# A gated mix of a convolution and a linear attention: data spectrum and parameters in memory of their own, attention values scaled in bf16 from on-chip memory, first query exponentials inside the key loop

## The chip, the cores and the metric

The kernel runs on one core of one Trainium2 chip. The metric is device time in microseconds; of three runs of the kernel before the change the median was 410.11 (406.83 to 412.22). The core's engines are named as in the profile: PE is TensorE's matrix multiply, PEld its weight load, DVE is VectorE, ACT is ScalarE, POOL is GpSimd, and SP is the engine whose queue issues the transfers. SBUF is the on-chip memory, PSUM the accumulators that PE writes, DRAM the memory off the core.

## The reference, cut to what matters

With x of 2048 rows and 512 channels, the output is `g*a + (1-g)*b`:

```python
g = sigmoid((x * gate_w).sum(-1, keepdims=True))
# a: a long convolution along the rows, per channel d
K = einsum("dn,dnl,dn->dl", Cc, exp(dt*A * l), dt*Bc).real      # n = 128 states, l = 0..2047
a = irfft(rfft(pad(x)) * rfft(pad(K)))[:2048] + x * Dskip
# b: linear attention, 32 heads of 16
q, k, v = x @ wqkv
phi(t) = concat(softmax(t @ w_phi), softmax(-(t @ w_phi)))
kv = einsum("hsf,hsd->hfd", phi(k), v);  z = phi(k).sum(s)
b = (phi(q) @ kv / (phi(q) @ z + 1e-6)) @ wo
```

Here `dt = exp(log_dt)`, and `A`, `Bc`, `Cc` are complex, each from two 512x128 inputs.

## The kernel before, in words

Every stage is written out in Python, with tiles taken from pools; the framework's scheduler then fixes one issue order for each engine, places the tiles, and puts in the semaphore waits. An engine works through its list in that order: an instruction that waits holds up everything behind it on its engine.

**The front.** SP loads two parameters (`Are`, `Aim`), `log_dt`, then the data as `UD` (four transfers, L738), four more parameters, the small vectors, the qkv weights `wraw` (L747) and `wo_sb` (L748). `build_fft_consts` builds the twiddle tables `TB` and `W1`, and from `TB` by transposes on PE (L151) the inverse table `TI`; `build_selectors` builds `selE`. `compute_rates` takes the decay rates through DRAM (`pz`, `stat`). `turn_x` transposes the data to `xT`. `compute_polar` makes the tables `Ctab` and `Dtab`: products of the parameters, then logarithms and exponentials, then an arctangent and four rounds of `big_a`, `big_n`, `trg` (an argument reduced on DVE, an absolute value and two sines on ACT). `fold_projection` multiplies the key and the query weights with `w_phi` (`Wkp`, `Wqp`). `u_path` computes the data's spectrum `XU` in two halves: matmuls `psA` (L381), 8 evictions `XAu`, matmuls `psB` (L402), 8 evictions `XU`. The tile `XAu` lies in the pool `xau`, which is opened where `compute_polar`'s pool has been closed. `gates` makes the gate.

**The key loop**, eight calls of `key_step`, each for two blocks of 128 rows: `pk` matmuls (L576), four exponentials `Ek` on ACT, sums `Zk` on DVE, their logarithm and reciprocal on ACT, `vp` matmuls (L589), then on DVE `vr = vp * reciprocal` for both signs (L591), and 64 small matmuls `kvp` that accumulate over the loop. `fold_kv` turns the result into `Mw` (matmuls `ktp`, `mps`).

**The query blocks.** `query_exp` (matmuls `pq`, exponentials `Eq`) and `query_block` for four blocks of 512 rows: `zs`, a short chain of ACT and DVE steps (`lnZ`, `den`, `apm`), then four times `aexp` on PE, two products `Eq` on DVE, twelve matmuls `bps` (L680, L683), an eviction `bs` and its transfer to `bSd`.

**The convolution kernel and the Fourier blocks.** `kgen_tables(h)` (four `E`, a table load, four `cs`, a table load on ACT) and `kgen(h)` (per half six DVE products `A`, five `R`, 64 matmuls `kps`; then the eviction `KD`, 8 matmuls `psA`, two evictions `XA`) make one eighth of the channels, h = 0 to 7. Two of them feed one Fourier block `fft(Q)`, Q = 0 to 3, of four groups: 48 matmuls `psB` (L402), eviction `XK`, two DVE products `t`, 32 matmuls `psz` (L444), eviction `Z`. After every two groups `Z` goes to DRAM as `Zd` (L451), and comes back transposed as `ZT` (L455). `finish(Q)` makes two output tiles `psy`: two matmuls each from `bS` (L467), 32 from `ZT` (L471), a product `ot` on DVE, four transfers. `psB`, `psz` and `psy` share a PSUM pool `psF` of two buffers; `args`, `kps`, `psA` share `psP`, also two. The end of the program reads

```python
fft(0)
for Q in range(1, 4):
    for h in (2 * Q, 2 * Q + 1):
        if h + 1 < 8:
            tabs[h + 1] = kgen_tables(h + 1)
        kgen(h)
    fft(Q)
    finish(Q - 1)
finish(3)
```

Of the kernel before, what the change touches and what calls it, by code (L numbers as in the profile page):

```python
# [11 lines left out]
ALU = mybir.AluOpType  # L12
# [99 lines left out]
def build_fft_consts(nc, act, persist, tp, ps_pool, icol, ident):  # L112
# [3 lines left out]
    fc.TI = persist.tile([128, 16, 4, 64], BF16, name="TI")  # L116
# [28 lines left out]
    for h in range(4):  # L145
        ps = ps_pool.tile([128, 4, 2, 64], F32, name="tips", tag="pb")
        for r4 in range(4):
            for rpar in range(2):
                r = 2 * (4 * h + r4) + rpar
                for cs in range(2):  # L150
                    nc.tensor.matmul(ps[64 * rpar:64 * rpar + 64, r4, cs, :], lhsT=fc.TB[0:64, r, cs, :], rhs=ident[0:64, 0:64],  # L151
                                     start=True, stop=True, tile_position=(0, 64 * rpar))
        nc.vector.tensor_copy(out=fc.TI[:, 4 * h:4 * h + 4, 2:4, :], in_=ps[:])
    nc.vector.tensor_scalar(out=fc.TI[:, :, 0:2, :], in0=fc.TI[:, :, 2:4, :], scalar1=-1.0, scalar2=None, op0=ALU.mult)
# [11 lines left out]

def build_selectors(nc, persist, tp, icol):

    selE = persist.tile([128, 32, 64], BF16, name="selE")
    c32 = tp.tile([128, 32], F32, name="c32")  # L170
    iota_f(nc, c32[:], [[1, 32]])
    m32 = tp.tile([128, 32], BF16, name="m32")
    nc.vector.tensor_scalar(out=m32[:], in0=c32[:], scalar1=icol["p31"], scalar2=None, op0=ALU.is_equal)
    v64 = tp.tile([128, 64], F32, name="v64")
    iota_f(nc, v64[:], [[1, 64]])
    b64 = tp.tile([128, 64], BF16, name="b64")
    nc.vector.tensor_scalar(out=b64[:], in0=v64[:], scalar1=1.0, scalar2=-31.5, op0=ALU.mult, op1=ALU.add)
    nc.vector.tensor_tensor(out=selE[:], in0=m32[:].unsqueeze(2).to_broadcast([128, 32, 64]),
                            in1=b64[:].unsqueeze(1).to_broadcast([128, 32, 64]), op=ALU.mult)
    return selE  # L180
# [22 lines left out]
def compute_polar(nc, act, persist, tp, psP, rawd, ld_b, ident):  # L203
# [29 lines left out]
    for k, o in (("Are", are), ("Aim", aim)):  # L233
        ps = turned(psP.tile([128, W], F32, name=f"ps{k}", tag="pb"), k)
        nc.vector.tensor_tensor(out=o[:], in0=ps[:], in1=dt_[:], op=ALU.mult)
    m2 = T("m2"); s2 = T("s2")
# [187 lines left out]
def k_spectrum_inverse(nc, fc, XA, nd, tpool, XU, d0, Z, Zd, ZT, ps_pool, tag, ev, evz, ngr):  # L424

    ns = 512 // nd
    for rg in range(16 // ns):
        rh0 = rg * ns
        ps = fft_stage_b(nc, fc, ps_pool, XA, nd // 2, rh0, tag)
        XK = tpool.tile([128, ns, 2, nd], BF16, name="XK")  # L430
        ev(XK[:].rearrange("p s i (c e x) -> p (s i c) e x", e=2, x=16), ps[:].rearrange("p e s i (c x) -> p (s i c) e x", x=16))
        t12 = tpool.tile([128, ns, 2, nd], BF16, name="t12")
        t34 = tpool.tile([128, ns, 2, nd], BF16, name="t34")
        Us = XU[:, rh0:rh0 + ns, :, d0:d0 + nd]
        nc.vector.tensor_tensor(out=t12[:], in0=Us, in1=XK[:], op=ALU.mult)  # L435
        nc.vector.tensor_tensor(out=t34[:], in0=Us, in1=XK[:, :, ::-1, :], op=ALU.mult)
# [131 lines left out]
def key_step(nc, act, at, xT, Wkp, wraw, kwk, psA, kvp, s2):  # L568
# [12 lines left out]
    vr = kwk.tile([128, 2, 2, 16, 34], BF16, name="vr")  # L581
    act(out=Zk[:], in_=Zk[:], func=ACT.Ln)
    act(out=vr[:, :, :, :, 32:34], in_=Zk[:].rearrange("p u g (m h) -> p (u g) m h", h=2), func=ACT.Exp, scale=-1.0)
    for u in range(2):
# [3 lines left out]
        for kt in range(4):  # L588
            nc.tensor.matmul(vp[:], lhsT=xT[:, kt, ss], rhs=wraw[:, kt, 1024:1536], start=(kt == 0), stop=(kt == 3))  # L589
        for sg in range(2):  # L590
            nc.vector.tensor_tensor(out=vr[:, u, sg, :, 0:32].rearrange("p m (h e) -> p m h e", e=16),  # L591
                                    in0=vp[:].rearrange("p (m h e) -> p m h e", m=16, h=2),
                                    in1=vr[:, u, sg, :, 32:34].unsqueeze(3).to_broadcast([128, 16, 2, 16]), op=ALU.mult)
        for i in range(8):
            sg, m = i // 4, i % 4
            for pr in range(4):
                nc.tensor.matmul(kvp[32 * pr:32 * pr + 32, i, :], lhsT=Ek[:, u, sg, 128 * m + 32 * pr:128 * m + 32 * pr + 32],
                                 rhs=vr[:, u, sg, 4 * m + pr, :], start=(st == 0 and i == 0), stop=(st == 15),
                                 tile_position=(0, 32 * pr), skip_group_check=True)


def fold_kv(nc, at, kp, kvp, wo_sb, ident, psA, Mw):
# [3 lines left out]
    nc.vector.tensor_tensor(out=zj[:], in0=kvp[:, :, 32:34], in1=at.mask2[:].unsqueeze(1).to_broadcast([128, 8, 2]), op=ALU.mult)  # L606
    nc.vector.tensor_reduce(out=zcol[:], in_=zj[:], axis=mybir.AxisListType.X, op=ALU.add)
    for pr in range(4):
        rows = slice(32 * pr, 32 * pr + 32)
        nc.vector.tensor_tensor(out=at.KVbd[rows, :, 32 * pr:32 * pr + 32].rearrange("p n (h e) -> p n h e", e=16),  # L610
                                in0=kvp[rows, :, 0:32].rearrange("p n (h e) -> p n h e", e=16),
                                in1=at.mask2[rows, :].unsqueeze(1).unsqueeze(3).to_broadcast([32, 8, 2, 16]), op=ALU.mult)
# [15 lines left out]
def query_exp(nc, act, qp, psA, xT, Wqp, b):  # L628
    Eq = []
    for mp in range(2):  # L630
        e = qp.tile([128, 2, 2, 512], BF16, name="Eq", bufs=4)
# [56 lines left out]
def full_kernel(tc, A_u, A_A_re, A_A_im, A_B_re, A_B_im, A_C_re, A_C_im, A_log_dt, A_Dskip,  # L688
# [7 lines left out]
    with ExitStack() as ctx:  # L696
# [29 lines left out]
        wc = rawp.tile([128, 4, 16], BF16, name="wc")
        UD = up.tile([128, 64, 128], BF16, name="UD")
        wraw = kpool.tile([128, 4, 1536], BF16, name="wraw")
        wo_sb = kpool.tile([128, 4, 512], BF16, name="wo_sb")

        def load_raw(k, src):
            nc.sync.dma_start(out=rawd[k][:], in_=src.rearrange("(g p) n -> p g n", p=128))
        with nc.allow_non_contiguous_dma(reason="small"):
            load_raw("Are", A_A_re)
            load_raw("Aim", A_A_im)
            nc.sync.dma_start(out=ldc[:], in_=A_log_dt.rearrange("(g p) -> p g", p=128))
            for dj in range(4):
                nc.sync.dma_start(out=UD[32 * dj:32 * dj + 32, :, :], in_=x2d[:, 128 * dj:128 * dj + 128].rearrange("(q t) d -> q t d", t=64))  # L738
            nc.sync.dma_start(out=ld_b[:], in_=A_log_dt.partition_broadcast(128))
            load_raw("Cre", A_C_re)  # L740
            load_raw("Bre", A_B_re)
            load_raw("Cim", A_C_im)
            load_raw("Bim", A_B_im)
# [3 lines left out]
        nc.sync.dma_start(out=wraw[:], in_=B_wqkv.rearrange("(kt p) c -> p kt c", p=128))  # L747
        nc.sync.dma_start(out=wo_sb[:], in_=B_wo.rearrange("(kt p) c -> p kt c", p=128))  # L748
# [6 lines left out]
        fc = build_fft_consts(nc, act, persist, tp, ring, icol, ident)  # L755
        selE = build_selectors(nc, persist, tp, icol)
# [4 lines left out]
        stat = compute_rates(nc, act, persist, tp, rawd, ldc, dram)  # L761

        turn_x(nc, UD, xT, ident, ring, eva)
        at = attention_consts(nc, aq, icol, ident, gw, Dcol_b, wc)
        Wqp = aq.tile([128, 4, 512], BF16, name="Wqp")
        Wkp = kpool.tile([128, 4, 512], BF16, name="Wkp")
        wT = kpool.tile([128, 4, 512], BF16, name="wT")
        polar = compute_polar(nc, act, persist, tp, ring, rawd, ld_b, ident)
        C, D = next(polar)
# [3 lines left out]
        xau = pool(cu, "xau", side="right")  # L773
        evu = Evict(nc, "aav")
        fold_projection(nc, at, wraw, 512, wT, Wkp, ident, ring, evu)
        u_path(nc, fc, UD, xau, XU, ring, evu, 2)
        wT2 = xau.tile([128, 4, 512], BF16, name="wT2")
        fold_projection(nc, at, wraw, 0, wT2, Wqp, ident, ring, evu)
# [5 lines left out]
        kwk = pool(ck, "kwk", 2)  # L784
        epool = pool(ctx, "epool", side="right")

# [7 lines left out]
        kvp = psA.tile([128, 8, 34], F32, name="kvp", tag="acc", bufs=1)  # L794
        for s2 in range(8):
            if s2 == 6:
                tabs[0] = kgen_tables(0)
            key_step(nc, act, at, xT, Wkp, wraw, kwk, psA, kvp, s2)

        Mw = aq.tile([128, 8, 512], BF16, name="Mw")  # L800
# [32 lines left out]
        Eq = {b: query_exp(nc, act, qp, psA, xT, Wqp, b) for b in range(2)}  # L833

# [4 lines left out]
        Eq[2] = query_exp(nc, act, qp, psA, xT, Wqp, 2)  # L839
        query(1)  # L840
        kgen(0)
        Eq[3] = query_exp(nc, act, qp, psA, xT, Wqp, 3)
# [8 lines left out]
        tpool = pool(ctx, "tpool", 2)  # L851
# [5 lines left out]
        def fft(Q):  # L857
            Z = fpool.tile([128, 32, nd], BF16, name="Z")
            ZT = fpool.tile([128, 32, nd], BF16, name="ZT", bufs=2)
# [4 lines left out]
            k_spectrum_inverse(nc, fc, XAs.pop(Q), nd, tpool, XU, nd * Q, Z, Zd, ZT, ps, "fb", eva, eva if Q < 3 else ev, 2)  # L864
# [6 lines left out]
        for Q in range(1, 4):  # L871
            for h in (2 * Q, 2 * Q + 1):
                if h + 1 < 8:
                    tabs[h + 1] = kgen_tables(h + 1)
                kgen(h)
            fft(Q)
            finish(Q - 1)
# [55 lines left out]
```

## Time and profile before

| | us |
|---|---|
| median of three runs | 410.11 |
| the profiled execution | 412.23 |
| its span, first to last instruction | 410.5 |
| mean granted clock of PE | 0.763 of full speed |
| PE busy | 271.4 (66%) |
| DVE busy | 274.2 (67%) |
| ACT busy | 257.2 (63%) |
| moved by transfers | 21.54 MB |

No engine is busy for much over two thirds of the span, so the shares alone don't tell what bounds the kernel; the stages do. The boundaries used below are instants at which the next stage's first instruction starts on the engine that leads it: the first square of `compute_polar` on ACT at 32.4, the end of its last sine at 74.8, the first key exponential at 108.8, the first `lnZ` at 179.7, and the evictions `KD` of h = 1 at 247.3 and of h = 3 at 287.1. All the later `KD` on ACT start at 309.99, 328.85, 351.79 and 362.97 (h = 4 to 7).

### The profile page before, as it was taken

What the parts mean: (1) busy time and instruction counts of PE and PEld (TensorE: products, weight loads), DVE (VectorE), ACT (ScalarE), POOL (GpSimd) and SP (SyncE); (2) the same over time, 40 slices, a digit from 0 to 9 for tenths busy, and PEclk for the clock granted to TensorE, in tenths of its full rate; (3) what the DMA queues carried; (4) which work ended last, traced back from release to release, by engine and by line L of the source; (5) the groups of instructions that cost most, each with busy time, mean ns of one, the idle gap of its engine ahead of it and who ended that gap; (6) DMA issues with size and microseconds to landing.
All of it is one profiled execution on the core that took longest, in us unless ns stands there. A gap on an engine that the chain in (4) does not pass through costs nothing.

```text
span 410.5 us, 10580 instructions
## 1 busy us (share of the span) xinstructions
PE 271.4 (66%) x4712; PEld 164.5 (40%) x4712; DVE 274.2 (67%) x470; ACT 257.2 (63%) x335; POOL 7.2 (2%) x19
## 2 busy tenths in 40 slices
PE   0465100397997877879997999764876778767621
PEld 0354000386333322344453454552554346456401
DVE  8956667644477847943874379697959695925502
ACT  3589452888565494786549726979695979643000
POOL 6000000000000000000000000000000000000000
PEclk9985555589699989688999899886588656665555
DMA  9991000000000000000010011255000950045894
GB/s 128 170 277 30 2 0 0 1 3 3 0 2 2 4 0 2 2 1 27 27 40 14 26 40 40 54 104 105 2 3 6 236 71 2 3 155 83 153 187 95
DMA packets 56317, 21.54 MB, mean 52 GB/s; under 512 B 52048, under 2 KB 54736, under 8 KB 56272
## 3 DMA queue, kind: packets, MB, share of 16 engines
q1 hardware_dynamic: 56272, 20.87, 26.2%
q8 instruction: 37, 0.61, 0.6%
q14 instruction: 8, 0.07, 0.1%
HBM read 11.95 MB, written 8.91 MB: 51 GB/s over the span
## 4 chain that ended last, share of the span: by engine, by line
ACT 34%; PE 28%; DVE 24%; DMA 6%; issue 4%; SPq 2%; DVEq 0%; ACTq 0%
PE bps L680 6%; ACT E L96 5%; ACT cs L96 4%; ACT L91 3%; PE pk L576 3%; ACT Eq L96 3%; DMA UD<-in_A_u_dram 3%; PE psz L444 3%; ACT XK L70 2%; PE psB L402 2%; DVE vr L591 2%; DVE Eq L676 2%; ACT Ek L96 2%; ACT xT L70 2%; ACT Z L70 2%
## 5 line engine op out<-in xcount | busy, mean ns | idle before, releaser
L444 PE MATMUL psz<-t,TI 64*128 64x128 bf16 x512 | 28.7, 277 | 16.2 <-DVE t L435 12.6
L381 PE MATMUL psA<-W,UD 128*64 128x256 bf16 x128 | 12.2, 351 | 39.3 <-ACT XAu L70 34.8
L444 PEld LDWEIGHTS <-TI 64*128 64x128 bf16 x512 | 23.5, 124 | 28.0 <-issue 22.8
L680 PE MATMUL bps<-Mw,Eq 128*128 128x512 bf16 x128 | 33.6, 410 | 1.4 <-DVE Eq L676 1.1
L96 ACT ACTIVATE E<-args 128x1024 bf16<-128x1024 f32 x32 | 31.3, 1034 | 2.9 <-PE args L313 2.9
L676 DVE TENSOR_TENSOR Eq<-Eq,aexp 128x512 bf16<-128x512 bf16 x32 | 20.5, 684 | 18.7 <-PE aexp L673 18.7
L96 ACT ACTIVATE cs<-args 128x1024 bf16<-128x1024 f32 x32 | 30.7, 1037 | 0.1
L402 PEld LDWEIGHTS <-TB 64*64 64x64 bf16 x1152 | 23.0, 136 | 11.0 <-issue 6.8
L579 DVE TENSOR_REDUCE Zk<-Ek 128x64 f32<-128x1024 bf16 x16 | 19.3, 1215 | 12.1 <-ACT Ek L96 12.1
L381 PEld LDWEIGHTS <-UD 128*64 128x64 bf16 x128 | 10.7, 203 | 40.6 <-issue 40.5
L70 ACT CAST Z<-psz 128x1024 bf16<-128x1024 f32 x14 | 14.2, 1017 | 20.0 <-PE psz L444 16.2
L91 ACT ACT_TABLE_LOAD x20 | 25.7, 1283 | 1.1 <-PEq L917 0.7
L341 DVE TENSOR_TENSOR A<-Ctab,Dtab 128x1024 bf16<-128x1024 bf16 x32 | 21.6, 690 | 6.6 <-PE kps L368 6.6
L435 DVE TENSOR_TENSOR t<-XU,XK 128x1024 bf16<-128x1024 bf16 x16 | 11.0, 690 | 21.3 <-ACT XK L70 17.2
L313 PE MATMUL args<-selE,stat 64*128 64x512 bf16 x64 | 22.0, 448 | 4.8 <-ACT E L96 2.7
L591 DVE TENSOR_TENSOR vr<-vp,vr 128x512 bf16<-128x512 f32 x32 | 19.9, 684 | 6.3 <-ACT vr L96 6.3
L96 ACT ACTIVATE Ek<-pk 128x512 bf16<-128x512 f32 x32 | 17.4, 593 | 10.7 <-PE pk L576 10.7
L811 ACT CAST bs<-bps 128x512 bf16<-128x512 f32 x16 | 9.4, 586 | 22.8 <-PE bps L683 17.1
L368 PE MATMUL kps<-R,A 128*32 128x64 bf16 x1024 | 19.8, 234 | 5.1 <-ACT cs L96 3.5
L342 DVE TENSOR_TENSOR Atmp<-Ctab,Dtab 128x1024 bf16<-128x1024 bf16 x32 | 22.1, 691 | 0.3
L343 DVE TENSOR_TENSOR A<-A,Atmp 128x1024 bf16<-128x1024 bf16 x32 | 22.1, 690 | 0.1
L368 PEld LDWEIGHTS <-A 128*32 128x32 bf16 x1024 | 17.7, 151 | 10.3 <-issue 9.1
(199 smaller groups left out, 580.1 us busy)
## 6 DMA issues: line engine op xcount, KB each, us to landing
Zd<-Z SPq DMA_DIRECT2D x8, 512.0 KB, 4.5
ZT<-Zd SPq DMA_DIRECT2D x32, 128.0 KB, 5.0
UD<-in_A_u_dram SPq DMA_DIRECT2D x4, 512.0 KB, 9.4
bSd<-bs SPq DMA_DIRECT2D x16, 128.0 KB, 1.7
bS<-bSd SPq DMA_DIRECT2D x4, 512.0 KB, 3.8
out_dram<-ot SPq DMA_DIRECT2D x32, 64.0 KB, 3.2
wraw<-in_B_wqkv_dram SPq DMA_DIRECT2D x1, 1536.0 KB, 7.6
wo_sb<-in_B_wo_dram SPq DMA_DIRECT2D x1, 512.0 KB, 7.8
```

What stands on the lines that cost most here:

```text
L70: self.nc.scalar.copy(out=out, in_=in_)
L91: p = self.nc.scalar.preload_act_table_set(name)
L96: i = self.nc.scalar.activation(**kw)
L342: nc.vector.tensor_tensor(out=tmp[:], in0=Cb(i1), in1=Db(j1), op=ALU.mult)
L343: nc.vector.tensor_tensor(out=A[:, o], in0=A[:, o], in1=tmp[:], op=op)
L368: nc.tensor.matmul(kps[32 * dj:32 * dj + 32, g4, e, :], lhsT=A[:, ri, :, :, d].rearrange("p a b -> p (a b)"), rhs=R[:, ri, d, :], start=(r ...
L381: nc.tensor.matmul(ps[64 * e:64 * e + 64, i, :], lhsT=l[e], rhs=rhs, start=True, stop=True, tile_position=(0, 64 * e))
L402: nc.tensor.matmul(o, lhsT=fc.TB[rows, r, op, :], rhs=rhs, start=(op == 0), stop=(op == 2), tile_position=(64 * e, 64 * rpar), skip_group_ ...
L444: nc.tensor.matmul(psz[:, rpar, sl, :], lhsT=fc.TI[rows, rh0 + sl, b0:b0 + 2, :].rearrange("p a b -> p (a b)"), rhs=rhs, start=(op == 0), ...
L591: nc.vector.tensor_tensor(out=vr[:, u, sg, :, 0:32].rearrange("p m (h e) -> p m h e", e=16), in0=vp[:].rearrange("p (m h e) -> p m h e", m ...
L676: nc.vector.tensor_tensor(out=e, in0=e, in1=ps[:], op=ALU.mult)
L680: nc.tensor.matmul(ps[:], lhsT=Eq[m // 2][:, m % 2, sg, 128 * i:128 * i + 128], rhs=Mw[:, 4 * sg + m, :], start=(k == 0), stop=False, skip ...
```

## The change

It has these parts.

1. **Front.** The data `UD` is loaded first on SP; the six parameters are issued by ACT's queue. `xau` is opened ahead of `compute_polar`'s pool, in memory of its own, and `u_path` stands between the first part of `compute_polar` (which now yields after the products) and its logarithms. `turn_x` is evicted by ACT and DVE (pattern a, a, v) where it was ACT alone. The weights come as `wqk` and `wv`; ACT copies `wv` into another column order (`Wv`). `wo_sb` is loaded at the start of the key loop.
2. **Tables.** `selE` and `TI` are built where the key loop starts; `TI` is evicted four times by ACT, where it was DVE.
3. **Key loop.** ACT evicts `vp` to `vb` in bf16; one DVE product of 128x1024 from SBUF replaces two of 128x512 from PSUM. The small matmuls `kvp` read `vr` with a stride.
4. **Order.** `query_exp(0)` and `query_exp(1)` stand in the key loop ahead of steps 4 and 7, `kgen_tables(0)` ahead of step 5 (was 6).
5. **Fourier blocks.** `XK` and the products share four buffers with `Eq`; `ZT` has one buffer, not two; `finish(Q-1)` stands after `kgen(2Q)`, not after `fft(Q)`.

```diff
-def build_fft_consts(nc, act, persist, tp, ps_pool, icol, ident):
+def build_fft_consts(nc, act, persist, tp, icol):
...
-        nc.vector.tensor_copy(out=fc.TI[:, 4 * h:4 * h + 4, 2:4, :], in_=ps[:])
-    nc.vector.tensor_scalar(out=fc.TI[:, :, 0:2, :], in0=fc.TI[:, :, 2:4, :], scalar1=-1.0, scalar2=None, op0=ALU.mult)
...
+def build_inverse_table(nc, fc, pool, ps_pool, ident):
+    fc.TI = pool.tile([128, 16, 4, 64], BF16, name="TI")
+    for h in range(2):
+        ps = ps_pool.tile([128, 8, 2, 64], F32, name="tips", tag="pb")
...
+        nc.scalar.copy(out=fc.TI[:, 8 * h:8 * h + 8, 2:4, :], in_=ps[:])
+        nc.scalar.mul(out=fc.TI[:, 8 * h:8 * h + 8, 0:2, :], in_=ps[:], mul=-1.0)
...
@@ compute_polar
         nc.vector.tensor_tensor(out=o[:], in0=ps[:], in1=dt_[:], op=ALU.mult)
+    yield C, D
...
@@ key_step
-    vr = kwk.tile([128, 2, 2, 16, 34], BF16, name="vr")
+    vr = kwk.tile([128, 2, 2, 17, 32], BF16, name="vr")
...
-        for sg in range(2):
-            nc.vector.tensor_tensor(out=vr[:, u, sg, :, 0:32].rearrange("p m (h e) -> p m h e", e=16),
-                                    in0=vp[:].rearrange("p (m h e) -> p m h e", m=16, h=2),
-                                    in1=vr[:, u, sg, :, 32:34].unsqueeze(3).to_broadcast([128, 16, 2, 16]), op=ALU.mult)
+        vb = kwk.tile([128, 16, 32], BF16, name="vb")
+        nc.scalar.copy(out=vb[:].rearrange("p e h -> p (e h)"), in_=vp[:])
+        nc.vector.tensor_tensor(out=vr[:, u, :, 0:16, :], in0=vb[:].unsqueeze(1).to_broadcast([128, 2, 16, 32]),
+                                in1=vr[:, u, :, 16:17, :].to_broadcast([128, 2, 16, 32]), op=ALU.mult)
...
-                nc.tensor.matmul(kvp[32 * pr:32 * pr + 32, i, :], lhsT=Ek[:, u, sg, 128 * m + 32 * pr:128 * m + 32 * pr + 32],
-                                 rhs=vr[:, u, sg, 4 * m + pr, :], start=(st == 0 and i == 0), stop=(st == 15),
+                h = 8 * m + 2 * pr
+                nc.tensor.matmul(kvp[32 * pr:32 * pr + 32, i, :, :], lhsT=Ek[:, u, sg, 16 * h:16 * h + 32], rhs=vr[:, u, sg, :, h:h + 2],
...
@@ full_kernel
+        xau = pool(cu, "xau", side="right")
...
+        for dj in range(4):
+            nc.sync.dma_start(out=UD[32 * dj:32 * dj + 32, :, :], in_=x2d[:, 128 * dj:128 * dj + 128].rearrange("(q t) d -> q t d", t=64))
...
+                nc.scalar.dma_start(out=rawd[k][:], in_=src.rearrange("(g p) n -> p g n", p=128))
...
-        turn_x(nc, UD, xT, ident, ring, eva)
+        turn_x(nc, UD, xT, ident, ring, evu)
...
+        fold_projection(nc, at, wqk, 512, wT, Wkp, ident, ring, evu)
+        u_path(nc, fc, UD, xau, XU, ring, evu, 2)
+        next(polar)
         act.begin(TRIG)
         next(polar, None)
...
+        nc.scalar.copy(out=Wv[:].rearrange("p k (e h) -> p k e h", h=32), in_=wv[:].rearrange("p k (h e) -> p k e h", h=32))
...
+            if s2 == 4:
+                Eq[0] = query_exp(nc, act, eqp, psA, xT, Wqp, 0)
+            if s2 == 5:
                 tabs[0] = kgen_tables(0)
+            if s2 == 7:
+                Eq[1] = query_exp(nc, act, eqp, psA, xT, Wqp, 1)
...
-            ZT = fpool.tile([128, 32, nd], BF16, name="ZT", bufs=2)
+            ZT = fpool.tile([128, 32, nd], BF16, name="ZT")
...
                 kgen(h)
+                if h == 2 * Q:
+                    finish(Q - 1)
             fft(Q)
-            finish(Q - 1)
```

## Prediction

> **What bounds the kernel now.** I read the 40 slices first (each 10.26 us).
>
> ```profile
> PE   0465100397997877879997999764876778767621
> DVE  8956667644477847943874379697959695925502
> ACT  3589452888565494786549726979695979643000
> PEclk9985555589699989688999899886588656665555
> DMA  9991000000000000000010011255000950045894
> ```
>
> PE has a hole in slices 5 to 7; transfers are saturated in the first three slices and busy in the last four, where the engines are nearly idle. Next came the busy time of each engine in the nine stages.
>
> ```profile
> core 0: us, PE busy (x) PEld busy (x) DVE busy (x) ACT busy (x) POOL busy (x), PEclk, DMA share, GB/s
> 0.00:32.40 32.40, 11.41 (x168) 10.02 (x168) 26.13 (x70) 18.58 (x21) 7.18 (x19) 0.93 1.06 192
> 32.40:74.80 42.40, 5.76 (x48) 5.05 (x49) 27.38 (x53) 24.65 (x34) 0.00 (x0) 0.50 0.00 1
> 74.80:108.80 34.00, 27.05 (x601) 21.23 (x601) 17.83 (x20) 25.99 (x28) 0.00 (x0) 0.75 0.01 2
> 108.80:179.70 70.90, 58.36 (x752) 24.57 (x751) 52.20 (x80) 45.93 (x87) 0.00 (x0) 0.92 0.01 2
> 179.70:247.30 67.60, 62.30 (x680) 32.52 (x679) 41.43 (x75) 41.43 (x66) 0.00 (x0) 0.92 0.08 27
> 247.30:287.10 39.80, 27.45 (x644) 17.81 (x644) 33.08 (x57) 34.52 (x37) 0.00 (x0) 0.83 0.37 78
> 287.10:367.00 79.90, 58.28 (x1300) 37.87 (x1301) 61.73 (x102) 60.16 (x61) 0.00 (x0) 0.67 0.29 62
> 367.00:385.10 18.10, 14.37 (x386) 12.11 (x386) 9.72 (x12) 5.91 (x7) 0.00 (x0) 0.50 0.65 89
> 385.10:410.50 25.40, 6.38 (x134) 3.31 (x133) 4.71 (x4) 0.00 (x0) 0.00 (x0) 0.50 0.80 145
> ```
>
> In order: load; polar tables; data spectrum; key loop; query stage, bound by PE (62.3 of 67.6); tables of h = 2, 3 with the first Fourier block; h = 4 to 7 with two more; the last block; its way through DRAM. Last, the waits named the holes:
>
> ```profile
> PE psA L381 <- ACT XAu L70: 34.8, 2, 34.6
> PE psy L471 <- DMA ZT<-Zd: 8.0, 1, 8.0
> ```
>
> The columns are total, times and longest. The first lies at PE's hole: `u_path` waits for memory that the polar tables hold. The second is the end, which the chain shows as bare latency:
>
> ```profile
> 383.86 1.24 DVE Z L68
> ...
> 386.67 4.49 DMA Zd<-Z
> 394.19 6.79 DMA ZT<-Zd
> ```
>
> Below I follow five marks: first `Ek` (108.84), first `lnZ` (179.66), `KD` of h = 3 (287.1), R = the end of the last `XA` eviction (367.05), the end (410.5). Places come from the changed program's issue order, which stands fixed per engine; durations from this trace.
>
> **Front, −5.5 (−21 to +5).** *Load.* ACT issues six parameters before its first table; SP issued such a load in 0.44 to 0.81, so about 3 us, of which some 1.35 reach `TB`. `UD` landed at 18.19. Its issue starts 1.6 earlier, but 0.5 MB of parameters more than before now travel beside it; at slice 0's 128 GB/s that is 3.9. I put it at 20.5. `log_dt` is queued behind `UD`, `dt` comes at 19.5, `bre`, `bim` at 21.3.
>
> *A new wait.* `Wv`, one ACT copy of 128x2048 (about 2 us, two evictions of 1.02), stands behind the first `xT` eviction and waits for `wv`, the last load in the queue (about 26.5). Four more `xT`, then `wT`, `Wkp`, stand behind it on ACT. `xT` is complete near 34.6 (before 26.8).
>
> *What goes.* `u_path` no longer waits for the pool: its evictions start at 38.5, not 76.1, and mix with the polar logarithms. ACT's list from there to the table load after the last sine is 49.5 us of work, by the rows of these operations. But `TI`'s four evictions (4 x 1.02, now on ACT) stand ahead of the second `big_n`, and their `tips` stand on PE behind `gps` and `zps`, so behind the weights' folding: my walk has round 1 at 73.6, `TI` waiting to 81.4, round 2 at 84.4, rounds 3 and 4 at 92.7 and 98.9, the table load's end at 103.1, first `Ek` 103.3: −5.5. DVE's 3.17 for `TI` goes from a place ahead of `UD`'s landing, worth nothing; `selE` (2.28) now stands ahead of the first `Zk` there, which delays it to 107.4. Ends: all waits gone, 38.5 + 49.5 = 88, −21; an `xT` later still, +5.
>
> The trace has the transfers' share at 9, 9, 9 in the first slices, under one issuing queue. The Trainium skill (DMA: Bandwidth & Descriptors, "Issuing engines are not separate DMA queues") says that transfers issued by several engines share the same 16 engines and save issue time alone; that rule speaks against a gain from part 1's second queue. By it and by the row the front stays at −5.5; were the parameters free beside `UD`, it would be about −9.5.
>
> **Key loop, −1.8 (−8 to +3).** `vr` cost 32 x 0.684 = 19.9 on DVE. 16 products from SBUF, at `A`'s 0.690 for 128x1024 bf16, are 11.0 (at worst, were the broadcasts to double it, 21.9). `vb` is 16 casts at `bs`'s 0.586 = 9.4, on ACT. So DVE gains 8.9 and ACT, which also takes 16 `Eq` (7.95 for them all), becomes the longer list. From the first logarithm (109.8; before 113.4) to the last reciprocal ACT has `Ek` 14.6, `vb` 7.3, logarithms and reciprocals 5.2, `Eq` 7.95, `E` 7.6, `cs` 3.8, loads 2.6 = 49.0, about 14 more than before, and my walk finds 3.5 of waits: 162.3 (before 160.6, there paced by DVE and PE at 5.75 a step). Behind it `pq` (7.6, 170.5 to 178.1) no longer stands, and the `vr` are 1.2 shorter: first `lnZ` at 172.4, −7.3 in all. The strided `kvp` rows cost PE nothing at the row's 180 ns; twice that would be 8.9 on PE, covered by ACT's list, and if ACT is not the bound it is paid.
>
> **Query stage, +3 (0 to +5).** Fifteen products of `kgen(0)` (10.3 at 0.69) ran beside `pq`; now they fall between `query(0)`'s. DVE then needs 3.8 a block step against PE's 3.22.
>
> **h = 2, 3: 0.** The same work in the same order; `ZT`'s single buffer and the four shared buffers made no wait in the walk. Should they, 1 to 3 us, in the range.
>
> **h = 4 to R, −11 (−14 to −7).** Before, two Fourier blocks lay in these 79.9: `KD` to `KD` is 22.9 (with `fft(1)`), 18.9 (its last group and the wait for it), 22.9 (`fft(2)`), 11.2 (none), then 4.1 to R. Now `fft(1)` waits for `finish(0)`, placed after `kgen(4)`, to give `psF` back, and runs after `kgen(5)`; `fft(2)` waits likewise until after R. A round without a block is ACT's list: `KD`, two `XA`, four `E`, four `cs`, two loads = 13.1, and about 1.7 of waits for `psA` and `psy`. Rounds: 14.7, 15, 23.5, 11.5, and 4.1: 69.
>
> **Tail, +31.5 (+18 to +36).** Before, R to the last `Z` is 18 us: one block, its PE at half clock (14.4 of 18.1). Now two lie there. `finish(1)`'s `psy` holds one `psF` buffer, so `fft(2)`'s groups go one by one through the other: `psB` 1.07, `XK` 1.02, the first `t` 0.69, `psz` 1.89, `Z` 1.02 make 5.7; `psz` end at R + 9.4, 15.5, 21.0, 27.0, the last `Z` at 28.1. Then 32 `psy` of `finish(2)` stand on PE ahead of every `psz` of `fft(3)`, and wait for `ZT` of Q = 2: `Zd` (one half, 2.8) lands at 31, `ZT`'s issue ends at 33.1, it lands at 37. PE idles some 6.5 us with `fft(3)`'s `t` ready behind it. Then `psy` and four `psz` and `Z` as before (11.7): last `Z` at R + 50 to 52. From there to the end 25.4 as before, less up to 2 for a `Zd` alone: R + 75, where it was R + 43.5. `out` and `ZT` waits on SP are 12 us clear of this.
>
> Sum: 410.5 − 5.5 − 1.8 + 3 − 11 + 31.5 = 426.7 span, with 1.7 around it 428.4. The profiled execution (412.23) lies 2.1 over the median, so I take 427.
>
> **Rivals.**
> 1. *The second block costs PE's work only* (`finish(2)` does not stop PE, as `ZT` lands under `fft(3)`'s `psB`, or the groups overlap): tail 14.4 + 4 = +18.5, median 413. For: ACT and DVE are half idle there (5.9 and 9.7 of 18.1). Against: one free buffer, and `psy` ahead of `psz` in the order. Decides if `ZT` of Q = 2 lands before R + 31.
> 2. *The front runs at ACT's pace*: `tips` comes before round 2 asks for it, and `wv` early. Place: ACT between `XAu` and the last sine; price 15; decides if `TI` is evicted by 78. Median 411. For: PE is idle to 76 in the trace, so nothing old is in its way. Both 1 and 2: 398, faster; this is the other side.
> 3. *`wv` lands last and late*: `Wv` sits in ACT's list over the four `xT`; each us later is a us of the front, +10 gives 437. For: a 1.5 MB `wraw` took 7.6 to land in a saturated queue. Decides if `xT` is complete after 40.
> 4. *Part 3 saves nothing*: `vr` at 1.37 and PE's rows doubled put the loop at +3, in the range.
>
> **Numbers.** Forecast 0.56, rival 1 0.18, rival 2 0.10, both 0.08, rival 3 0.08. A difference under 2% (8.2 us) cannot be told from none in this kernel, whose three runs spread 1.3%. Faster, below 402: both rivals and the low ends of the one or other, 0.12. Within 2%, 402 to 418: the rest of rivals 1 and 2 and a little of the forecast, 0.24. Slower: 0.64. The range, 408 to 439, leaves out the joint rival and the far ends; the forecast's own is 418 to 434.
>
> **What would show it.** `Wv` idle before its start near 24 to 26; `big_n` waiting on `TI`; first `Ek` near 103 (88 for rival 2); first `lnZ` near 172; `KD` 14 to 15 apart from h = 3 to 5; four `XK` between h = 5 and 6 and eight after the last `XA`; PE waiting 6 to 7 us for `ZT` in mid-tail; last `Z` 50 us after R. It would be wrong if more than four `XK` stand between h = 3 and R, or if that PE wait is absent.

## The result and the profile after

The changed kernel is slower: 425.39 us median of four runs (423.42 to 425.77), against 408.47 for four runs of the kernel before; ratio 1.039 (95% interval 1.030 to 1.049). Its profiled execution has a span of 423.5, 13.0 more than before's 410.5; the profiled execution of the kernel before is the slowest of its four, so the medians lie 16.9 apart where the profiles show 13.0. The slices, in the same rows as before:

```profile
PE   1148664803888793699988987647769665662701
DVE  6487747577743448569745898939889872242402
ACT  2579998647779892855488279598888832350100
PEclk9999897675999695869999997775555885565565
DMA  9980001000000000000100111580000382166193
```

PE's hole in slices 5 to 7 is gone; a shorter one lies in slices 9 and 10, among the rounds of sines. A new thin stretch stands at the end: in the last seven slices DVE and ACT have 4 and less but for one, and PE its pauses. The stages, cut at the marks (the first row is the whole front, the last two are the way from R to the end, cut at the last `Z`):

```profile
core 0: us, PE busy (x) PEld busy (x) DVE busy (x) ACT busy (x) POOL busy (x), PEclk, DMA share, GB/s
0.00:101.10 101.10, 45.72 (x819) 37.92 (x821) 66.92 (x134) 71.25 (x81) 4.76 (x19) 0.86 0.36 62
101.10:174.10 73.00, 56.53 (x741) 24.33 (x748) 40.38 (x56) 55.84 (x106) 0.00 (x0) 0.85 0.01 2
174.10:243.40 69.30, 61.21 (x670) 32.35 (x679) 49.62 (x90) 41.20 (x67) 0.00 (x0) 0.93 0.08 26
243.40:285.10 41.70, 28.58 (x646) 18.67 (x648) 32.84 (x57) 34.58 (x37) 0.00 (x0) 0.82 0.43 87
285.10:351.90 66.80, 47.76 (x975) 28.95 (x977) 56.71 (x95) 52.69 (x53) 0.00 (x0) 0.60 0.24 49
351.90:402.90 51.00, 28.08 (x771) 23.79 (x774) 17.52 (x22) 14.00 (x15) 0.00 (x0) 0.57 0.33 72
402.90:423.50 20.60, 2.70 (x66) 1.68 (x65) 2.45 (x2) 0.00 (x0) 0.00 (x0) 0.58 0.74 134
```

Set against before, by the marks of the prediction (each a difference of two starts on ACT, or of an end):

| stage | before | after | difference | forecast |
|---|---|---|---|---|
| front, to the first `Ek` | 108.84 | 101.11 | −7.7 | −5.5 |
| key loop, to the first `lnZ` | 70.82 | 72.99 | +2.2 | −1.8 |
| query stage to `KD` of h = 3 | 107.41 | 111.00 | +3.6 | +3 |
| `KD` of h = 3 to R | 79.97 | 66.83 | −13.1 | −11 |
| R to the end | 43.46 | 71.57 | +28.1 | +31.5 |
| span | 410.5 | 423.5 | +13.0 | +16.2 |

The loss is the last row, which the row above it only half gives back. PE's timeline shows how `psy` came to stand there (start, duration, instruction, and in brackets the idle time before it and its releaser):

```profile
275.08 0.59 PE L471 MATMUL psy<-bS,ident 128*128 128x512 bf16 x2 [0.24 <-ACT Z L70]
...
312.94 1.04 PE L475 MATMUL psy<-ZT,TJ 64*32 64x128 bf16 x32
...
315.70 1.06 PE L406 MATMUL psB<-XA,TB 64*64 64x128 bf16 x48 [1.04 <-DVE ot L478]
...
388.18 1.04 PE L475 MATMUL psy<-ZT,TJ 64*32 64x128 bf16 x32 [7.80 <-DMA ZT<-Zd]
390.55 1.89 PE L448 MATMUL psz<-tt,TI 64*128 64x128 bf16 x32 [1.33 <-DVE ot L478]
```

At 275 the `bS` matmuls of `finish(0)` take the `psF` buffers, and the matmuls from `ZT` follow at 312.9. `ZT`'s last loads were issued from 278.43 to 280.33, and such a load landed in 4.8 (median; 6.6 at most), so the data lay there from about 285: for some 28 us `psy` kept both buffers although its data were there, and the Fourier block of Q = 1 stood behind it: its first `psB`, at 315.70, is released by the product `ot` that frees the first of them. In the tail it is a wait for data, and PE itself stands in it: 32 `psy` wait 7.80 us for `ZT` of Q = 2, and the first `psz` of `fft(3)` comes after them. Before, `psy` waited once for `ZT`, 8.0 us at the very end; now it waits three times, 7.80 in mid-tail, then 10.42 and 0.87 at the end:

```profile
PE psy L475 <- DMA ZT<-Zd: 19.1, 3, 10.4
```

### The profile page after: what moved, and what is told of

The parts are those of the page before. It is cut to its first block, busy times and chain, and to the rows that moved or that the text cites. A ratio compares the mean times of both kernels' runs of the same rounds, so it can differ in the third digit from the quotient of the medians.

```text
span 423.5 us, 10570 instructions
## 1 busy us (share of the span) xinstructions
PE 270.6 (64%) x4688; PEld 167.7 (40%) x4712; DVE 266.4 (63%) x452; ACT 269.6 (64%) x353; POOL 4.8 (1%) x19
## 3 DMA queue, kind: packets, MB, share of 16 engines
q1 hardware_dynamic: 53632, 20.08, 23.5%
## 4 chain that ended last, share of the span: by engine, by line
DVE 32%; ACT 26%; PE 26%; DMA 7%; SPq 5%; issue 3%; ACTq 0%; DVEq 0%
PE bps L684 6%; PE psz L448 4%; ACT E L96 4%; DVE A L345 3%; DMA ZT<-Zd 3%; ACT cs L96 3%; DVE A L347 3%; DVE Eq L680 3%; ACT XAu L70 2%; DVE Atmp L346 2%; SPq L725 2%; PE pq L640 2%; DVE Zk L583 2%; DVE R L358 2%; ACT L91 2%
## 5 line engine op out<-in xcount | busy, mean ns | idle before, releaser
L448 PE MATMUL psz<-tt,TI 64*128 64x128 bf16 x512 | 29.2, 284 | 19.6 <-DVE tt L439 13.9
L448 PEld LDWEIGHTS <-TI 64*128 64x128 bf16 x512 | 24.5, 127 | 24.4 <-issue 22.9
L593 PE MATMUL vp<-Wv,xT 128*128 128x512 bf16 x60 | 17.7, 419 | 20.8 <-ACT Ek L96 20.1
L406 PEld LDWEIGHTS <-TB 64*64 64x64 bf16 x1152 | 24.0, 138 | 16.4 <-issue 13.6
L583 DVE TENSOR_REDUCE Zk<-Ek 128x64 f32<-128x1024 bf16 x16 | 18.8, 1212 | 18.2 <-ACT Ek L96 18.2
L478 DVE TENSOR_TENSOR ot<-psy,gT 128x1024 bf16<-128x1024 f32 x8 | 9.8, 1222 | 31.1 <-PE psy L475 31.1
L317 PE MATMUL args<-selE,stat 64*128 64x512 bf16 x64 | 22.9, 464 | 6.0 <-ACT cs L96 2.6
L372 PEld LDWEIGHTS <-A 128*32 128x32 bf16 x1024 | 18.2, 152 | 17.8 <-issue 14.7
L439 DVE TENSOR_TENSOR tt<-XU,XK 128x1024 bf16<-128x1024 bf16 x16 | 11.0, 689 | 21.5 <-ACT XK L70 19.4
L70 ACT CAST XK<-psB 128x1024 bf16<-128x1024 f32 x16 | 16.2, 1020 | 10.6 <-PE psB L406 8.6
L346 DVE TENSOR_TENSOR Atmp<-Ctab,Dtab 128x1024 bf16<-128x1024 bf16 x32 | 21.9, 686 | 0.2
L347 DVE TENSOR_TENSOR A<-A,Atmp 128x1024 bf16<-128x1024 bf16 x32 | 21.9, 685 | 0.1
L475 PE MATMUL psy<-ZT,TJ 64*32 64x128 bf16 x256 | 8.3, 307 | 19.1 <-DMA ZT<-Zd 19.1
## 6 DMA issues: line engine op xcount, KB each, us to landing
UD<-in_A_u_dram SPq DMA_DIRECT2D x4, 512.0 KB, 11.5
```

The lines of the kernel that those rows point to most:

```text
L70: self.nc.scalar.copy(out=out, in_=in_)
L346: nc.vector.tensor_tensor(out=tmp[:], in0=Cb(i1), in1=Db(j1), op=ALU.mult)
L347: nc.vector.tensor_tensor(out=A[:, o], in0=A[:, o], in1=tmp[:], op=op)
L372: nc.tensor.matmul(kps[32 * dj:32 * dj + 32, g4, e, :], lhsT=A[:, ri, :, :, d].rearrange("p a b -> p (a b)"), rhs=R[:, ri, d, :], start=(r ...
L406: nc.tensor.matmul(o, lhsT=fc.TB[rows, r, op, :], rhs=rhs, start=(op == 0), stop=(op == 2), tile_position=(64 * e, 64 * rpar), skip_group_ ...
L448: nc.tensor.matmul(psz[:, rpar, sl, :], lhsT=fc.TI[rows, rh0 + sl, b0:b0 + 2, :].rearrange("p a b -> p (a b)"), rhs=rhs, start=(op == 0), ...
```

## The experiments

Marks of every profiled run, in us, worked out as above:

| run | first `Ek` | to `lnZ` | to `KD` h = 3 | to R | to the end | span |
|---|---|---|---|---|---|---|
| before | 108.84 | 70.82 | 107.41 | 79.97 | 43.46 | 410.5 |
| changed | 101.11 | 72.99 | 111.00 | 66.83 | 71.57 | 423.5 |
| e1 | 102.69 | 73.39 | 106.68 | 78.59 | 58.55 | 419.9 |
| e2 (on before) | 106.77 | 68.83 | 110.38 | 74.18 | 73.24 | 433.4 |
| e3 | 99.27 | 72.55 | 109.14 | 66.82 | 72.32 | 420.1 |
| e4 | 100.82 | 72.40 | 110.86 | 66.84 | 71.48 | 422.4 |
| e5 | 101.33 | 72.08 | 109.77 | 78.77 | 48.05 | 410.0 |
| e6 | 101.69 | 73.21 | 126.67 | 103.44 | 35.29 | 440.3 |
| e7 (on e5) | 101.83 | 71.67 | 108.31 | 78.73 | 48.26 | 408.8 |
| e8 (on e5) | 101.54 | 78.66 | 109.92 | 78.30 | 46.68 | 415.1 |
| e9 (on e5) | 101.64 | 74.20 | 109.34 | 79.99 | 46.73 | 411.9 |
| e10 | 99.95 | 72.35 | 110.27 | 66.42 | 71.61 | 420.6 |
| e11 | 100.84 | 71.66 | 108.31 | 78.76 | 45.23 | 404.8 |
| e12 | 113.04 | 68.37 | 110.92 | 66.81 | 72.66 | 431.8 |

A mark of one execution holds to about 2 us: e2's front has before's instructions in before's order, and its first `Ek` comes 2.1 earlier (from 76.1 to 106.7 the granted clock was 0.88 there, 0.78 in the kernel before). The seven runs that have the changed front unaltered put the first `Ek` at 101.11 to 102.69.

**e1, `finish` back.**

```diff
-        opool = pool(ctx, "opool", 2)
+        opool = pool(ctx, "opool", 1)
...
+            ZT = fpool.tile([128, 32, nd], BF16, name="ZT", bufs=2)
...
                 kgen(h)
-                if h == 2 * Q:
-                    finish(Q - 1)
             fft(Q)
+            finish(Q - 1)
```

> The changed kernel with finish(Q-1) behind fft(Q) again; for that ZT has two buffers again and ot one instead of two (memory); XK and the products still share four buffers with Eq. Theory (the early finish orders fft(2) behind the last XA, and everything else in the changed kernel costs or gains little): KD of h = 3 to R back to 79 to 80 us (66.8 in the changed kernel), R to the end back to 43 to 45 (71.6), span 408 to 411, the time within 1% of the kernel before. Rival A (the four shared buffers or the load in the front set the end): R to the end stays over 55, span over 418. Rival B (only ZT's one buffer did it): cannot be told from the theory by this run, but by e2.

420.25 us, ratio 1.025 (1.020 to 1.031). R to the end fell from 71.6 to 58.6, not to 44, and the span is 419.9: the theory's numbers failed, and rival A's (over 55, over 418) came. Its reason did not: the longest wait but one points to another cause, the edit's own:

```profile
DVE ot L478 <- DMA out_dram<-ot: 27.8, 5, 10.8
```

With one `ot` buffer each output product waits for the transfers of the one before. e5 has two `ot` buffers again and keeps what rival A blamed, and there the tail is 48.05.

**e2, the early `finish` alone, in the kernel before** (the diff of the change's last part but for `ZT`).

> The kernel before with finish(Q-1) after kgen(2Q) and nothing else; ZT keeps two buffers, XK and the products their own pool. Theory (the place of finish alone makes the loss): KD of h = 3 to R 66 to 69 (79.9 before), R to the end 70 to 76 (43.5), so +14 to +17: span 424 to 428, ratio 1.035 to 1.04. Rival B (ZT's one buffer or the shared buffers make it): span under 414, ratio under 1.01.

433.93 us, ratio 1.058 (1.050 to 1.066). The place of `finish` alone makes the loss, with two `ZT` buffers and with `XK` and the products in a pool of their own: rival B falls. Its tail is 73.2, as expected, but its rounds became only 5.8 us shorter where the changed kernel's became 13.1 shorter (74.2, expected 66 to 69), so in the kernel before the edit costs 22.9 of span, more than the whole change and more than the theory's 14 to 17. The round with `fft(1)` took 26.1 there, 21.9 in the changed kernel; why was not tried.

**e5, `finish` back with memory to spare.**

```diff
+        def bring(Q):
+            Zd, bS = outs[Q]
+            ZT = fpool.tile([128, 32, nd], BF16, name="ZT")
...
+                        nc.sync.dma_start(out=ZT[p0:p0 + 16, :, :], in_=Zd[ri, 32 * th:32 * th + 32, r0:r0 + 16, :].rearrange("t r d -> r t d"))
...
             fft(Q)
+            finish(Q - 1)
+            bring(Q)
```

> The changed kernel with finish(Q-1) behind fft(Q) again, two ot buffers and one ZT buffer, as in the change; ZT's loads are issued behind finish(Q-1), so that one buffer is enough. Theory (e1's last 15 us were its single ot buffer, for which DVE waited 27.8 us; the rest of its loss is none): R to the end 43 to 46 (58.6 in e1, 71.6 in the changed kernel), KD of h = 3 to R 78 to 81, first Ek 101 to 103, span 403 to 410, within 2% of the kernel before. Rival A (the shared buffers or one ZT cost the tail): R to the end over 52, span over 415.

412.46 us, ratio 1.014 (1.002 to 1.026), span 410.0. The rounds cost their 78.8 again and the tail 48.05. Rival A falls. That undoes 13.5 of the changed kernel's span, and the change's loss was 13.0: what is left of the change wins nothing in the profiles, and by the medians it is 1.4% slower than the kernel before. The tail missed the theory's 43 to 46 by 2. The 4.6 by which it misses before's 43.5 lie behind the last `Z`: `ZT`'s loads are issued from 391.64, 11.8 after the last `Z`, where before had 391.18 and 6.1. Of these 5.7, some 3.1 came with the first half of `Zd`, which stands on SP behind the loads of the `ZT` before and landed 9.2 after the last `Z` (before 6.1), and 2.6 with the eight outputs that stand between. Issued by ACT's queue (e11) they leave a tail of 45.2.

**e6, the early `finish` with `psy` in the other PSUM pool.**

```diff
-            k_out(nc, fc, ident, ZT, nd, nd * Q, bS, gT, out2d, opool, psF, "fb")
+            k_out(nc, fc, ident, ZT, nd, nd * Q, bS, gT, out2d, opool, psP, "pb")
```

> The changed kernel with finish where the change put it, but its psy tiles taken from psP, so that they hold no buffer of psF. Theory (the early finish costs because psy holds psF until ZT is there, and the Fourier groups wait): the Fourier blocks come back among the rounds h = 4 and h = 6, KD of h = 3 to R 78 to 86 (66.8), R to the end 43 to 50 (71.6), span 408 to 418. Rival D (the place in the order itself makes it: psy's wait for ZT stands ahead of other work on PE): R to the end over 60, span over 420.

442.20 us, ratio 1.084 (1.075 to 1.093), the slowest of all: the theory's number was wrong, and half of its reason right. Rival D's span came (over 420), its tail (over 60) did not. The Fourier blocks are back among the rounds, and R to the end is 35.3, less than in any other run. But the tables now pay. PE's and ACT's timelines at the first of the three places:

```profile
282.10 1.04 PE L475 MATMUL psy<-ZT,TJ 64*32 64x128 bf16 x32 [8.51 <-DMA ZT<-Zd]
...
285.51 1.02 ACT L96 ACTIVATE E<-args 128x1024 bf16<-128x1024 f32 x1 [11.41 <-PE args L317]
```

`psy` holds both buffers of `psP` until `ZT` has come back from DRAM; `args`, `kps` and `psA` live there, so ACT stands 11.41 us, and the four `E` behind run one at a time. PE's own wait of 8.51 lies in this too: the `args` stand behind `psy` in its list, which is rival D's reason, and the run does not part the two. Of the rounds, those with `psy` took 37.7, 33.7 and 18.2 between their `KD`, against 20.3, 15.0 and 11.2 in the changed kernel. In both pools the cost is the time from `psy`'s first matmuls to its last; the pool decided who waited.

**e7, the query exponentials behind the key loop.**

```diff
-            if s2 == 4:
-                Eq[0] = query_exp(nc, act, eqp, psA, xT, Wqp, 0)
...
+        for b in range(2):
+            Eq[b] = query_exp(nc, act, eqp, psA, xT, Wqp, b)
         query(0)
```

> e5 with query_exp(0) and query_exp(1) behind the key loop, as in the kernel before. Theory (the key loop is bound by ACT, 50.3 of 61.9 us, so its 16 Eq cost their 8 there, and give 7.6 of pq back behind it, with products of kgen(0) beside it): first Ek to first lnZ within 2 of e5 (73), first lnZ to KD of h = 3 2 to 4 less than in e5, the time 1 to 4 us below e5. Rival E (ACT is not the bound, the Eq were free in the loop): first Ek to first lnZ 6 to 8 more than in e5, the time 3 to 6 above it.

411.63 us against e5's 412.46, 1.2 of span: no difference that can be told. Rival E would have put 6 to 8 us on the key loop, which came 0.4 shorter. To the end of the last reciprocal it is 7.5 shorter (50.4, 57.9 in e5), and from there to the first `lnZ` 7.1 longer: the `Eq` and `pq` cost in the loop what they cost behind it. The place of the two `query_exp` in part 4 of the change is worth nothing either way; that of `kgen_tables(0)` was not tried.

**e8 and e9, what `vb` is worth.**

```diff
-        vb = kwk.tile([128, 16, 32], BF16, name="vb")
-        nc.scalar.copy(out=vb[:].rearrange("p e h -> p (e h)"), in_=vp[:])
-        nc.vector.tensor_tensor(out=vr[:, u, :, 0:16, :], in0=vb[:].unsqueeze(1).to_broadcast([128, 2, 16, 32]),
+        nc.vector.tensor_tensor(out=vr[:, u, :, 0:16, :], in0=vp[:].rearrange("p (e h) -> p e h", h=32).unsqueeze(1).to_broadcast([128, 2, 16, 32]),
```

> e5 without vb: the one product of 128x1024 a block reads vp from PSUM, so ACT loses 16 casts (9.5 us in the changed kernel), and DVE's 16 products take about 1.22 as other such products from PSUM do, not 0.69 (+8.5). Theory (ACT bounds the loop): first Ek to first lnZ 66 to 70 (73 in the changed kernel), the time 3 to 7 us below e5. Rival F (DVE bounds it as in the kernel before, and the bf16 copy pays): first Ek to first lnZ 73 to 77, the time not below e5.

416.90 us; the key loop took 78.66, 6.6 more than in e5. My theory falls: ACT lost its casts, and the loop grew, by more than rival F's range too. Rival F's reason had then to be told from another, which e9 did (e5 with `vb` in `F32`):

> e5 with vb in 32 bits instead of bf16: ACT's casts and the early release of vp's PSUM buffer stay, and only DVE's 16 products read a wider operand. Theory G (e8 lost 6.6 us in the key loop because vp kept one of the three PSUM buffers shared with pk until the reciprocal was there): first Ek to first lnZ 71 to 74.5 (72.1 in e5, 78.7 in e8), whatever the products take. Rival F (DVE's products at 1.22 instead of 0.69 lost it): first Ek to first lnZ 77 to 80, if the products take 1.2 here too. If they take 0.7, the run says nothing against F but that bf16 isn't needed for it.

413.00 us; the key loop took 74.20. The lines of both, e8 first, then e9 (busy and mean, and after the bar the idle time before and its releaser):

```profile
L590 DVE TENSOR_TENSOR vr<-vp,vr 128x1024 bf16<-128x1024 f32 x16 | 18.9, 1220 | 6.6 <-ACT vr L96 4.2 <-PE vp L589 1.7 <-PE pq L634 0.7
L96 ACT ACTIVATE Ek<-pk 128x512 bf16<-128x512 f32 x32 | 17.4, 623 | 8.5 <-PE pk L576 8.5
L96 ACT ACTIVATE Eq<-pq 128x512 bf16<-128x512 f32 x16 | 8.2, 607 | 4.4 <-PE pq L634 4.4
```

```profile
L592 DVE TENSOR_TENSOR vr<-vb,vr 128x1024 bf16<-128x1024 f32 x16 | 18.9, 1221 | 8.9 <-ACT vr L96 8.9
L96 ACT ACTIVATE Ek<-pk 128x512 bf16<-128x512 f32 x32 | 17.6, 602 | 2.5 <-PE pk L576 2.3 <-PE kvp L598 0.2
```

The products take 1.22 in both, and ACT has 9.5 more to do in e9, yet e9 is 4.5 shorter. In e8 ACT waits 8.5 for `pk` and 4.4 for `pq`; in e9 2.3. `pk`, `vp` and `pq` share three PSUM buffers, and in e8 `vp` keeps its own until the reciprocal is there. Up to the last reciprocal e5, e8 and e9 took 57.9, 63.2 and 58.2 us: the 5.3 that e8 loses there come back with the early release of PSUM, net of ACT's casts, whatever the product takes. The wider operand shows behind it, where `KVbd` begins 1.1 later in both, as the last two products take 0.53 more each. So of the 6.6 that `vb` saves in the changed layout, 4.5 go with the early release; the other 2.1, e9 against e5, are hardly more than a mark's 2 us.

**e3, e4, e10, e12, the front.** e3 puts the copy `Wv` on GpSimd (`nc.gpsimd.tensor_copy`), e4 `TI`'s evictions on DVE, e10 loads `wv` into the memory that `XAu` gives back (`wv = xau.tile([128, 4, 512], BF16, name="wv", tag="XAu")`), e12 moves `xau` and `u_path` back behind `compute_polar`.

> The changed kernel with the copy Wv on GpSimd instead of ACT. Theory (the copy's 3.9 us and its 1.8 us wait for wv stand on the path of the front, over the xT evictions): u_path's first eviction 4 to 5.7 us earlier (38.2 in the changed kernel), the first Ek at 96 to 98 (101.1), span 418 to 420. Rival C (the rounds of sines wait for DVE or for tips, whatever xT does): first Ek within 1 us of 101.1. If GpSimd's copy is not done by 95, the key loop's first vp waits for it.

> The changed kernel with TI's four evictions on DVE instead of ACT, in the same place. Theory (TI, waiting for tips, held up round 2's big_n on ACT, which was ready on DVE at 79.1 and began at 82.2): first Ek 2 to 4 us earlier, 97 to 99, the span 420 to 422. Rival C (DVE's own list sets the rounds, and TI lengthens it): first Ek no earlier than 100.5, or later.

> The changed kernel with wv loaded into the memory that XAu gives back, so that ACT's copy Wv comes after the data spectrum, not between the xT evictions. In e3 GpSimd's copy stretched a product on DVE (cbi, 3.19 instead of 0.68), so that run did not show the whole of it. Theory (5.7 us of wait and copy stand on the front's path): u_path's first eviction at 33 to 36 (38.2 in the changed kernel), first Ek at 96.5 to 99.5 (101.1). Rival C (the front waits for the products and for PE there, whatever ACT does): u_path's first eviction no earlier than 37, first Ek no earlier than 99.5 but for the place of the copy among the sines.

> The changed kernel with the data spectrum's memory taken back: xau is opened where compute_polar's pool is closed and u_path stands there, as in the kernel before; the loads, Wv, TI on ACT and all else stay as changed. Theory (the wait for that memory was worth more than the front's gain of 7.7 shows, the copy Wv and TI's evictions on ACT having taken some of it back): u_path's first eviction near 78 to 82 (76.1 before, 38.2 changed), first Ek 111 to 118 (108.84 before, 101.1 changed), span 432 to 441. Rival H (the front's gain comes from the loads and from DVE's lighter list, and the wait for the memory was covered): first Ek under 106, span under 429.

One execution each, of 422.04, 424.14 and 422.67 us: e3 brought the first `Ek` to 99.27, e4 to 100.82, e10 to 99.95 (101.11 in the changed kernel): 1.8, 0.3 and 1.2 us, of 3 to 5, 2 to 4 and 1.6 to 4.6 expected, so e3 and e10 ended between theory and rival, and e4 with rival C. All three lie within the 2 us of a mark. In e3 `u_path`'s first eviction came 0.9 earlier (37.37; 4 to 5.7 expected), behind a product on DVE that took 3.19 beside the copy. Taking away `Wv`'s 1.8 of wait and 3.9 of copy moved `u_path`'s first eviction only from 38.24 to 36.10 (e10): PE's `xps` for the third `xT` then wait 1.67 for the products on DVE, whose PSUM they need. Nor does e10 show the whole of the copy: the first `big_n` came 3.1 earlier (68.85, 71.96 in the changed kernel), but then the copy stood on ACT ahead of the second, which came only 1.1 earlier:

```profile
77.28 3.88 ACT L777 COPY Wv<-wv 128x2048 bf16<-128x2048 bf16 x1
81.06 1.06 ACT L282 ACTIVATE big_n<-big_a 128x1024 f32<-128x1024 f32 x1
```

In e4 round 2's `big_n` began 2.9 earlier, at 79.27, as the theory had it, but DVE evicted the rest of `TI` ahead of the next `big_a`, and round 3 began at 90.22 where it was 90.51. After the data spectrum the front is a chain of four rounds between ACT and DVE: in the changed kernel ACT waits 4.43 and 3.27 us for `big_a` in the last two. e12 took 433.59 us (ratio 1.065, 1.055 to 1.076): first `Ek` 113.04, and the old wait is back:

```profile
PE psA L385 <- ACT XAu L70: 43.0, 3, 42.6
```

So the memory of its own is worth 11.9 at the first `Ek` and 8.3 of span, and the other edits of the front cost 4.2 where it is not there (113.04 against before's 108.84); of these, `TI`'s four evictions take 3.6, as there they stand on ACT directly ahead of the first `Ek` (109.41 to 113.04). The span, 431.8, came 0.2 below the range of the theory, as the key loop was 4.6 shorter there. Its issue order has the first `E` in the loop's first steps; whether that is why was not tried.

**e11, together:** e5 with e10, e4, e7, and the last `ZT`'s loads on ACT's queue.

> e5 with Wv late (e10), TI evicted by DVE (e4), the query exponentials behind the key loop (e7), and the last ZT's loads issued by ACT's queue, not behind the outputs on SP. By the sums of the single runs: first Ek at 97 to 99, to the first lnZ 71 to 73, to KD of h = 3 108, to R 78.7, to the end 43 to 46, so a span of 398 to 405 and a time 1 to 3% below the kernel before. If the gains of the front are the same wait seen twice, the span is 405 to 408, no difference that can be told.

407.50 us (12 runs) against 410.65 for the kernel before; ratio 0.994 (0.990 to 0.997). Faster than the kernel before, by less than 2%, and by less than the 1 to 3% expected; the span, 404.8, is within the 398 to 405. The front gave less than its single runs (100.84, expected 97 to 99), and the tail gave what was expected (45.23).

## Why the prediction was right, and where it was off

**The forecast case came true.** 427 was said, 425.39 measured, and it is the tail. The signs came too: behind `KD` of h = 3 there are four `XK` between h = 5 and h = 6 and eight after the last `XA`, and no others. That the total came so near is partly luck: the five terms missed by −2.2, +4.0, +0.6, −2.1 and −3.4 us, which nearly cancel.

**Tail, +31.5 forecast, +28.1 measured.** Up to the last `Z` the walk held: R + 51.0, forecast 50 to 52. PE waited 7.80 for `ZT` of Q = 2, which landed at R + 36.3 (forecast 6.5 and 37). Rival 1 needed it before R + 31, and fell there. From the last `Z` it took 20.6 instead of 23.4 to 25.4. Of the 4.8 less than before, 1.8 are the last `Zd`, which landed in 2.72 where before's had 4.49, and these the forecast had as "up to 2"; it did not have the 1.6 by which that `Zd` was issued sooner after `Z`, nor the 1.2 less from the last `ZT`'s landing to the end. Before, the load of `bS` was issued half a microsecond ahead of the `Zd`, here 23 us; that this made the difference was not tried.

```profile
378.95 3.44 DMA Zd<-Z
382.81 5.32 DMA ZT<-Zd
...
402.83 2.72 DMA Zd<-Z
409.14 6.61 DMA ZT<-Zd
```

These are the chain's links through DRAM, in order of time: two crossings end to end, where the kernel before had one on its chain.

**h = 4 to R, −11 forecast, −13.1 measured.** The rounds came at 14.7, 15.0, 21.9, 11.2 and 4.1 (forecast 14.7, 15, 23.5, 11.5, 4.1). The text put `finish(0)` behind `kgen(4)`; in the program it stands behind `kgen(2)`, and it is the issue order that brought its last matmuls into the round after `kgen(4)`. That order was fixed before any run, so why it was laid out for a `ZT` 28 us later than the real one stays open.

**Front, −5.5 forecast, −7.7 measured.** The walk put each mark some 2 us too late, by the same amount from the second round on (84.4, 92.7, 98.9, 103.3 forecast):

```profile
26.22 3.92 ACT L777 COPY Wv<-wv 128x2048 bf16<-128x2048 bf16 x1 [1.79 <-DMA wv<-in_B_wqkv_dram]
...
38.24 5.60 ACT L70 CAST XAu<-psA 128x1024 bf16<-128x1024 f32 x6
...
79.48 1.01 ACT L166 CAST TI<-tips 128x1024 bf16<-128x1024 f32 x1 [3.68 <-PE tips L164]
...
82.20 1.08 ACT L282 ACTIVATE big_n<-big_a 128x1024 f32<-128x1024 f32 x1
...
101.11 2.04 ACT L96 ACTIVATE Ek<-pk 128x512 bf16<-128x512 f32 x4
```

`Wv` waited for `wv` to 26.2 as said, but took 3.92, not 2; with the copy moved behind `u_path` (e10), 1.2 was left at the first `Ek`. `TI` came at 79.5, not by 78, so rival 2 fell. But `TI` on ACT did not decide: on DVE (e4) it leaves 0.3 at the first `Ek`. The row of the transfers' share, 9, 9, 8, was full again with two issuing queues, and the first `xT` came at 23.42 us; no run shows the load gaining from the second queue.

**Key loop, −1.8 forecast, +2.2 measured: the step that failed.** Up to the end of the last reciprocal the sum held: 58.6 us after the first `Ek` (59.0 forecast), with `vr` at 0.688, `vb` at 0.609 and ACT busy 50.3 of these 58.6. Behind it came 14.4 us to `lnZ` instead of 10.1. The prediction priced the new column order in `vr` and `kvp`, but not in `fold_kv`, where four products `KVbd` now write pairs of elements that lie 16 apart. The tile and ACT's wait behind it, before and then after:

```profile
L610 DVE TENSOR_TENSOR KVbd<-kvp,mask x4: 401/419/429, 163.6 to 164.9; 32x256 bf16<-32x256 f32 x4
ACT KVT L621 <- PE ktp L620: 5.6, 1, 5.6
```

```profile
L614 DVE TENSOR_TENSOR KVbd<-kvp,mask x4: 1272/1291/1302, 161.7 to 165.6; 32x256 bf16<-32x256 f32 x4
ACT KVT L625 <- PE ktp L624: 8.0, 1, 8.0
```

Four times 0.87 more is 3.5 us, alone on the path: `ktp` waits for it, and ACT for `ktp` (7.98, which would be longer still had `KVbd` not begun 1.0 sooner behind the reciprocal). Most of the other 0.8 lies in the `mps`, which now alternate with `zs` on PE, so that ACT waits 0.9 for them. This is read from the rows; no run gave `KVbd` its old layout back. A second reason was wrong though its sum held: `vb` was costed as DVE's gain and ACT's loss. e8 and e9 show that its worth lies mostly in the PSUM buffer it frees. That ACT's list is what bounds the loop is supported but not shown: e7 took 8 us of `Eq` off it, and the way to the last reciprocal became 7.5 shorter, but the `pq` left PE's list with them.

**Query stage, +3 forecast, +3.6 measured**, with 49.6 of DVE work where 41.4 was. **Rival 4** fell with `vr` at 0.688, half of the 1.37 that it asked for. **Rival 3** asked for `xT` complete after 40; the last eviction ended at 35.1.

## What to carry to other kernels

A step whose last input comes back from DRAM holds whatever it has taken, its PSUM buffers and its place in the engine's list, from the moment its first input is ready; put it where its last input is due, and ask of every earlier place who needs those buffers, or stands behind it in the list, meanwhile. A copy out of PSUM can pay by the buffer that it frees even where it makes no engine faster, so look for the buffer's next user before pricing the copy by engine time. When a layout changes, price every instruction that reads or writes it, the few small ones on a serial stretch too.

## What the runs showed of the hardware

With the copy `Wv` on GpSimd (e3), one DVE product beside it took almost five times its usual time, in one execution. GpSimd's and DVE's timelines of e3:

```profile
26.23 3.92 POOL L777 COPY Wv<-wv 128x2048 bf16<-128x2048 bf16 x1 [21.14 <-DMA wv<-in_B_wqkv_dram]
```

```profile
26.92 0.68 DVE L238 TENSOR_TENSOR are<-psAre,dt 128x512 f32<-128x512 f32 x1
27.52 3.19 DVE L234 TENSOR_TENSOR cbi<-cbi,bre 128x512 f32<-128x512 f32 x1
30.63 0.68 DVE L238 TENSOR_TENSOR aim<-psAim,dt 128x512 f32<-128x512 f32 x1
```

`are`, with one input in PSUM, ran at 0.68 beside the copy; `cbi`, with both inputs in SBUF, took 3.19 (0.68 in the changed kernel, where ACT makes the copy) and ended at 30.71, where the copy ended at 30.15. This agrees with the Trainium skill (GPSIMD Engine Reference, section "Specifications"), which says that GpSimd shares its SBUF interfaces with VectorE and contends with its instructions that have two SBUF inputs. Here the product lasted through the rest of the copy.

A copy of 128x2048 that reads elements 16 apart took 3.92 us on ACT, nearly twice what two evictions of 128x1024 from PSUM take (1.01 each); `KVbd`, which writes pairs of elements 16 apart, took 3.1 times its former time on DVE with the same 256 elements a row. Neither was run with its layout alone changed, so that the step is the reason is not shown.
